# One subtraction of the first stage on VectorE instead of GpSimd, with the order of TensorE's groups written out anew

## The chip, the cores and the metric

The kernel runs on one core of one Trainium2 chip. The metric is the device time of one execution in microseconds. Comparisons are made with the median of several runs. TensorE is called PE, VectorE DVE, ScalarE ACT, GpSimd POOL and SyncE SP, as in the profile.

## The reference

One layer normalisation of `x` (2048 rows of 640) feeds attention with 32 heads of 20, and a parallel branch does a shifted mixer and an MLP:

```python
xn = _layernorm(x)
qkv = (xn @ wqkv) ...                       # q, k, v: 32 heads of 20
p = softmax(q @ k.T * 20 ** -0.5)
attn = (p @ v) @ wo
h  = gelu(_layernorm(x) @ w1)               # then its four column blocks are shifted by +1, -1, +2, -2 rows
x1 = x + shifted(h) @ w2
mlp = gelu(_layernorm(x1) @ w3) @ w4
out = x + attn + x1 + mlp
```

All of it is in float32.

## The kernel before

**Two parts for every factor.** To keep float32 precision with PE's faster reading of rounded values, each matmul factor is held as a high part (the rounded value) and a low part (the value minus the high part). A product is the sum of high times high, high times low and low times high. So each weight tile costs a copy that rounds it and a subtraction that makes the low part.

**The plan.** The Python code first lists all operations with an engine, an estimated cost, dependences and a key (a due time; the smallest ready key goes first on an engine). `Plan.schedule` then runs a list scheduler over them, and the instructions are emitted in its order, so each engine's queue has that order. An operation with `port=True` also takes a resource that the planner lends to DVE or POOL, one at a time, for the operation's planned length. PE's queue is ruled further by a string, `ORDER`, with one letter for each PE group: `m` for the score products whose row maxima are taken (two matmuls, tile `pm`, then two maxima on DVE, tile `mx`), `s` for the score products that go to the exponential (two matmuls, tile `s`, then two exponentials on ACT, tile `p`), `p` for the product of the exponentials with v (tile `pv`, eight matmuls), `d` for everything else (projections, mixer, MLP, transposes). The letters say which kind comes next; among the `d` groups the planner's keys decide. The string has 65 rows and 7059 letters: 4499 `d`, 1024 `m`, 1024 `s`, 512 `p`.

**The first stage** works on four blocks `tb` of 512 rows of `x`. For a block `norm_rows` takes the statistics of its four row tiles on DVE (`bn_a`, `mva`), then the inverse root on DVE and POOL (`rv_a` on DVE; `ry_a`, `rt_a`, `lnk` on POOL), and normalises the tiles in place, two on DVE and two on ACT (`xb`). The first block does this in two halves. `turn_tiles` transposes the tiles on PE (`tp`), copies the high part on ACT and subtracts on DVE to make the low part (`xT`). Then `twins` multiplies the first columns of the q and k weights with the block, the k sum on one half of PE's rows and the q sum on the other, in two turns; in the second turn the halves are swapped. Each turn has 15 pairs of matmuls: five with high weights and high rows, five with high weights and low rows, five with low weights. Between the turns stands a fence: a memset of a one-element tile (`scratch`, line 344) on POOL that waits for the end of the first turn and lets the second begin. The two sums go through ACT and DVE (`hl`), are placed by PE (`pk`) and stored.

**The weights of the first stage.** `load_w0` loads the first 128 columns of the k weights (`w_k`, e = 1) and of the q weights (`w_q`, e = 0), 640x128 held as 128x640, rounds them on ACT and makes the low part with a subtraction of two 128x640 operands. `split_wv` does the same for the first half of the v weights in five pieces (`wv`). `norm_rows` ties these low parts behind DVE's normalising of row tile 2 (`pl.behind`). On POOL the five `wv` subtractions have key -903, those of `w_k` and `w_q` -898. Four memsets (`vst`, key -140) fill gaps on POOL from there on.

Of the kernel before, what the change touches and what calls it, by code (L numbers as in the profile page):

```python
# [97 lines left out]
ORDER = (  # L98
    "dddddddddddddddddddddddddddddddddddddddddddddddddddddddddddddddddddddddddddddddddddddddddddddddddddddddddmmddd"
    "ddddddddddddddddddddddddddddddddddddddddddddddddddddddddddddmdddddddmddddmddddmddddmddddddmdddddddddddddddmddd"  # L100
    "dddmmdddddddmdddddmddddddddmdmddddddddddddddddddmdddddddddmdmmdddddddddddddddmdddddddddddmddddmmdddddddddddddd"
    "mdddddmddddddddmdddmmdddddddddddddddddddddmddddddddmdmmdddddddmddddddddddddddddddddmddmddmdddddddmdddddddddddd"
    "mdddddddddddsmmdddddddddddsddsdddddddsdmdddddddddmssddddddddmdsdddsdddmdddddsdmdsddppppddmsddmddsdmdsddsddmdds"
    "dddsdmdmddppppmddddmsdddsddddmdsdddsmdddsdmdsddddsmddsddmddmmppppmdsdddsdsdmdddmdsddmdddsmddddsdmddsdmddsddmdm"
    "ddmdpppsmspsmsmspmsmpsmspmsmpsmssmpmsmpsmddddsmddddmdddsdmdddsmdddsdmdddsdmddsdmddmddsppssmpsmmppmdddsddmddsdd"
    "dmddddmdspddmsdddddsdmdsdddddmddmppsmddddddddsmdddddddsmdddddsddmdddsddddmdmppmsdddddsddmdsddddmdddsmddddddsdm"
    "ddddsdddmdmppppsmddddsddmddsddddsdddmsddddddmsddddmdddddsmpmsmpppdsmdddsddddddmsdddddsmddddsddmddsdddmdddmdspp"
    "ppdmdsmdddddddsddmdddddmsddddddmsdddsdddmdddmppsdmdddddsdmddddsddmddsdmdddsdddmddsdddddmdmppsmdddddsdmddsddddd"
    "ddmsmdddddddsddddmddmddmppmsmppmdsdsdddmdsddddmsdddddmmsdddddddmsdddsddmsdddsppmspsmsddpdssmpdddppsddsddmdddsd"
    "ddsdmddddsmdddmddsdddmddsddmdddsppmmspppdmsddddmsdddsdmdsdddddmsmdddsdddmdsddsdddmddmdsppmsmsppmsdddmmpdpdsmdd"  # L110
    "ddmdsdddmddsddmddsdmdsdddmdsdddsddmddsddspsmpmspdmspdppdmdsddmddddmddddsdddsmddsddmddsdddsmdsddmddsdmppppmsddm"
    "dddddmsdddmdsdmdddsmddddmsdddmddsdmdddsddmppsmmppmsddddsdsmddddsdmddsdddmsddmddsdmdddspsmpsdmdddmdsddddsmppdmm"
    "sdpdpsdddsdsdddddmsddddsdddmsddddmdsddddmdsdddmddsppmmsmspppsmspsmddddmdsdmdddmddsddddmsdddmsddddmsdddmdsdddmd"
    "mppssppsmdddddpssmpmdddsdmdddsdmdddsddddsmddddmdsdddmdddsddsddmpppmsmpdddsmddddmddmddsdddddmsddddmdsddddmsdddd"
    "ddsmsmpsmpppsmspsddmdpmdsddmdsdddmsdddddmssdddddmddmdsddsddmddsdpsmmpppsdmddddsmdsdddmdsddmddsdsppppmsdddmsddd"
    "msdddmdsddmdddssdddddpsmmppmddsdmddmdddddsdmpdmsdddsdmsdddmdsddmddsdmdddsddsdmppppmsdddmdsddsddsdmddddddmsmddd"
    "ddddsmddddmsddsddmsmmpppmspsmspsmddddsmdddsdmpsmddddmddsdmdsddddmspsdmpsmdddsdddmsddsdmdddddmddsppppddsmddsddm"
    "dddsmddsddmdsdmddsddmdsdmddmdmppppssddmddddmsdddmdsdddddmsmddddsddmdddsmdddsddmdmppppmsddmdsdddmdsddmddsddmdds"
    "mdddmdsdddsdsddmpsmpsmpsmpmsddmdsddddsdddsdmdmdpppdsddmddsdddsmpmsddmdsddmdsdddsddmsdddmdsppsmmppmsdddmdsddmdd"
    "ddmdsddddmsmdddddsmddddmdsdddmddspsmmpppmdddmddsdddmsddddmsdddmsddmdsdddmddmsddddsdmddspmspssmpsmspsmsdpsmspms"  # L120
    "mpmspssmpssmpssmpmsspsmpssmpsmmppmsddddmddddmdddddddmmdddddsdddddddddddddddmsddsddddddddssdddmddddddmdsdddddsd"
    "dddmdmppppmdddsdddddddsmdmddddddsddmddddsdddddddddddddddsddddddddddddmsmddddddsddddmddddddddsddmddddddmddddspp"
    "ppdmdsddddsddddmsddddsdddddddddddddsdddddsdddmsddddddmmdddddddsdddmdddmddppdsppmdddddsdmddsddddddsmdsddddddsdd"
    "mdddddsdmppsdmddddddsdmdddddsddmpdmsddddddmddsddddddmspsmpsmspssmppsddddddddddddddddddddsspmmspsmmppmmddsddddd"
    "dmdddmsddddsmdmddddddmsdddmdsdddmddddmdsddmdddmsdddmddddsmddddmdsdmddddspppppmsdddddddmddsddmddsddmddsdddsmddd"
    "sddmddsddsddmddddmmppppmsdddmdddddsdmddsdmdddsmdddsdmdddsdmdddsdmdddsmpppmsdddsdmdsdddmdsdddmsdddsmdsddddmmppp"
    "msdpsmddsddmdsddmddsdmpppsmdddsdmdddsdmdddsdmdddsmdddsdmddsdmddsdmddsdddmmppppmdddmddddsddmddsddddssdddmdddsds"
    "ddmdddsddsdspppsmspmmsppsmdddsdmdddsdmdddsdmdddsmdddsdmdddsddmddsdddmdspdppmsddmdsdddmsddmdsddmdsdddmmppppmsdd"
    "sddmdsdddmdsdmdddsdddddmddddmmdddddddsmdppsdmdddsdmddsddsddmdddsdmpsmspssmppppmsddmdsddddmsdmdddsddmddsmdddsdm"
    "ddddsmddsddmdddmsppppdmdsdmdddsdmdddmdsdddddssmdddddsddmddsdmdddddsmmmppmpmmspsmspsmspsmspsmspsmspsmspssmpmsmp"  # L130
    "ddddsmdddmdddsdddddsmdddsdddmddmppsmdddddddddddsdddsdddmdddddsmddddddddsdddmddddddddsdddddmdddspmddsdpdsmdsddd"
    "ddddmddddmmdddddddddddddpppddmdddddddsddddddsmddddddmddddmdddddspsmdddsddddmddsddsddddmsdddddmddsdddmdddsddddd"
    "dddddddppppmsdddddmsddddsdmdddddsmdddddmsdddmddddddmdspmsppddmsdddddddmsddddddsdmddddddsdmddddddmdspdmdsddmddd"
    "ddsddddddmmdddddsddddddsddddmsppdmsmppsmspssmpmsspmsspmsddddddddssddddddddddddpmspssmpsmspsmspsmspsmdddddsspps"
    "sddddmdsddddmdmmddddddmdddmdddddddddmdddddmdddddddmsdddmdddmddddmdsddmdddddmddmddddmdsdddddmmddddsddmddsdppdmd"
    "dsddddmmpppmddsddmdddddmddsdmdddsmdddsdmddsdmddsdmddsddmdsppsmspppsmdddsdmdddsdmdddsdmdddsmdddsddmddsddmddsdds"
    "ddmpppssmpppmsddsddmddsddmddsdmddddsmdsdddmddsdmddddsmddddmsppppddmdmdddsddddsdmdsddddmsddmddsdsddddmsdddmdmdd"
# [1427 lines left out]
```

## Time and profile before

| | |
|---|---|
| median of three runs | 1871.93 us (1871.77 to 1875.42) |
| the profiled execution | 1870.62 us, of which the span is 1868.5 us |
| granted TensorE clock | 0.999 |
| PE | 1855.8 us busy, 99% of the span |
| DVE | 1550.7 us, 83% |
| ACT | 1337.8 us, 72% |
| POOL | 404.8 us, 22% |

The span runs from the first to the last instruction. In the views, a row of the timeline gives start and length in us, the engine, the line of the kernel, the operation, the tile written and the tile read, and in brackets how long the engine was idle before it and what ended that. The chain of waits follows the last instruction back to whatever released it, so its pieces add up to the span. Most operations are recorded at line 324, matmul groups at line 356, because a helper issues them.

### The profile page before, as it was taken

The page shows a single profiled execution, that of the slowest core. Times are in us where ns is not written, and L with a number is a line of the kernel's source. Part 1 is how long each engine was busy: PE and PEld are TensorE (multiplying, and loading weights), DVE is VectorE, ACT ScalarE, POOL GpSimd, SP SyncE. Part 2 cuts the span into 40 slices and gives each one's busy share as a digit, 9 for nine tenths or more (in the row PEclk, how much of TensorE's full clock was granted, in tenths as well). Part 3 has the DMA queues.
Part 4 walks back from the last instruction along what each step waited for, and adds up shares of the span by engine and source line. Part 5 has one row for each costly group of instructions (what it writes and reads, how often), then busy time and mean ns, then how long its engine had stood idle before and what let it go on. Part 6 is the DMA issues. An engine that isn't in the chain of part 4 may idle for free.

```text
span 1868.5 us, 44324 instructions
## 1 busy us (share of the span) xinstructions
PE 1855.8 (99%) x17233; PEld 1276.6 (68%) x17233; DVE 1550.7 (83%) x2739; ACT 1337.8 (72%) x2459; POOL 404.8 (22%) x620
## 2 busy tenths in 40 slices
PE   9999999999999999999999999999999999999998
PEld 7975776666666648676666756665776777775777
DVE  8989888888888999988788988778887888789724
ACT  5267777787877886677887677788677777778661
POOL 6001111321212213211213320111222122212211
PEclk9999999999999999999999999999999999999999
DMA  5664555536353475645345673434423242343402
GB/s 200 178 184 134 136 136 158 162 115 180 107 158 122 123 243 169 189 151 177 118 127 187 210 208 102 126 98 151 121 80 91 73 116 84 81 135 121 139 13 113
DMA packets 230360, 257.79 MB, mean 138 GB/s; under 512 B 60520, under 2 KB 175672, under 8 KB 228352
## 3 DMA queue, kind: packets, MB, share of 16 engines
q1 hardware_dynamic: 230152, 254.98, 45.7%
q8 instruction: 135, 2.21, 0.5%
q14 instruction: 73, 0.60, 0.1%
HBM read 151.64 MB, written 103.25 MB: 136 GB/s over the span
## 4 chain that ended last, share of the span: by engine, by line
PE 95%; DVE 2%; POOL 1%; DMA 1%; issue 0%; SPq 0%; ACT 0%; DVEq 0%; POOLq 0%; ACTq 0%
PE ps L356 26%; PE pv L356 25%; PE s L356 14%; PE pm L356 14%; PE psv L356 4%; PE pso L356 3%; PE ps_k L356 3%; PE ps_q L356 3%; DVE mx L324 1%; PE psl L356 1%; PE tz L324 1%; DMA wd_w<-ph_w 0%; PE pmt L356 0%; PE c_w L356 0%; PE tp L324 0%
## 5 line engine op out<-in xcount | busy, mean ns | idle before, releaser
L324 DVE TENSOR_REDUCE mx<-pm 128x1 f32<-128x512 f32 x2048 | 1282.2, 683 | 207.9 <-PE pm L356 192.9
L324 ACT ACTIVATE p<-s 128x512 f32<-128x512 f32 x2048 | 1080.8, 611 | 277.4 <-PE s L356 232.7
L356 PE MATMUL pv<-p,v 128*32 128x512 f32 x4096 | 493.7, 598 | 0.1
L356 PE MATMUL s<-zq,kpack 62*128 62x512 f32 x2048 | 443.4, 410 | 0.7
L356 PE MATMUL pm<-kpack,zq 60*128 60x512 f32 x2048 | 441.0, 409 | 1.6 <-DVE ob L324 1.6
L356 PE MATMUL ps<-xT,w_w 64*128 64x512 f32 x2040 | 322.8, 394 | 0.4 <-DVE mx L324 0.3
L356 PEld LDWEIGHTS s<-zq,kpack 62*128 62x128 f32 x2048 | 227.4, 185 | 128.2 <-ACT p L324 38.6
L356 PEld LDWEIGHTS pm<-kpack,zq 60*128 60x128 f32 x2048 | 228.3, 185 | 110.6 <-DVE mx L324 26.3
L356 PEld LDWEIGHTS pv<-p,v 128*32 128x32 f32 x4096 | 110.2, 109 | 225.0 <-issue 196.1
L356 PEld LDWEIGHTS ps<-xT,w_w 64*128 64x128 f32 x2040 | 212.9, 186 | 32.9 <-issue 2.1
L324 POOL TENSOR_TENSOR ob<-ob,obq 128x512 f32<-128x512 f32 x96 | 125.2, 1304 | 403.2 <-ACT obq L324 312.3
L356 PE MATMUL ps<-xT 64*128 64x320 f32 x1632 | 168.0, 307 | 0.0
L356 PEld LDWEIGHTS ps<-xT 64*128 64x128 f32 x1632 | 150.2, 186 | 9.0 <-issue 2.5
L356 PE MATMUL ps<-xT,gT 64*128 64x320 f32 x1152 | 119.1, 307 | 0.0
L324 ACT COPY obq<-pv 128x512 f32<-128x512 f32 x75 | 44.1, 588 | 103.8 <-PE pv L356 102.8
L356 PEld LDWEIGHTS ps<-xT,gT 64*128 64x128 f32 x1152 | 104.4, 186 | 6.2 <-issue 0.8
L344 POOL MEMSET scratch<- 1x1 f32 x134 | 12.1, 90 | 432.0 <-PE ps L356 206.3
L356 PE MATMUL psv<-wv,xT 64*128 64x320 f32 x960 | 92.1, 309 | 1.0 <-ACT xT L324 0.8
L356 PEld LDWEIGHTS psv<-wv,xT 64*128 64x128 f32 x960 | 80.9, 185 | 7.4 <-POOL scratch L344 1.2
L356 PE MATMUL ps_q<-xT,w_q 64*128 64x512 f32 x480 | 77.9, 393 | 0.0
L356 PE MATMUL ps_k<-xT,w_k 64*128 64x512 f32 x480 | 74.4, 394 | 0.0
L324 POOL TENSOR_TENSOR ph_w<-pr_w,ph_w 128x320 fp32r<-128x320 f32 (+2 forms) x48 | 36.7, 764 | 151.6 <-ACT ph_w L324 120.9
(171 smaller groups left out, 1360.9 us busy)
## 6 DMA issues: line engine op xcount, KB each, us to landing
zq<-qd SPq DMA_DIRECT2D x156, 80.0 KB
kpack<-kd SPq DMA_DIRECT2D x78, 160.0 KB
w_w<-wd_w SPq DMA_DIRECT2D x48, 256.0 KB
gd<-pre SPq DMA_DIRECT2D x8, 1536.0 KB
g<-gd SPq DMA_DIRECT2D x64, 192.0 KB
wd_w<-ph_w SPq DMA_DIRECT2D x34, 320.0 KB
xT<-wd_w SPq DMA_DIRECT2D x34, 320.0 KB
vd<-vst SPq DMA_DIRECT2D x32, 256.0 KB
```

The costliest lines, as they stand in the source:

```text
L324: o.insts = [getattr(e, m)(val(out), *[val(x) for x in ins], **{k: val(v) for k, v in kw.items()})]
L344: o.insts = [nc.gpsimd.memset(scratch.get(), 0.0)]
L356: o.insts = [nc.tensor.matmul(out.get(), lhsT.get(), rhs.get(), **kw) for out, lhsT, rhs, kw in products]
```

## The change

The subtraction that makes the low part of `w_q` is given to DVE instead of POOL, with DVE's planned cost; that of `w_k` stays on POOL. The key, the port flag and the tie behind the normalising of row tile 2 stay.

```diff
-        w0s.append(pl("pool", c_pool(640), "tensor_sub", w0[e][:, 1], raw, _f(w0[e][:, 0]), port=True))
+        w0s.append(pl("pool" if e else "dve", (c_pool if e else c_dve)(640), "tensor_sub", w0[e][:, 1], raw, _f(w0[e][:, 0]),
+                      port=True))
```

The planned costs are `c_pool(640)` = 2.11 * 640 + 145 = 1495 ns and `c_dve(640)` = 640 / 0.96 + 65 = 732 ns.

`ORDER` is also written out anew: 18 of its 65 rows differ. The counts of the four letters are the same; groups change places by a few letters. The first 232 letters are unchanged, and so are those from 640 to 1399 and all from 3900 on; the differences lie in between, most of them in letters 232 to 640 and 2420 to 2860. The first of the rows that differ and one from the middle, as examples:

```diff
-    "dddmmdddddddmdddddmddddddddmdmddddddddddddddddddmdddddddddmdmmdddddddddddddddmdddddddddddmddddmmdddddddddddddd"
...
+    "dddmmddddddddmddddmdddddmddddmddddddddddddddddddmdmdddddddddmmddddddddddddddmddddddddddddmddddmmdddddddddddddd"
...
-    "mpmspssmpssmpssmpmsspsmpssmpsmmppmsddddmddddmdddddddmmdddddsdddddddddddddddmsddsddddddddssdddmddddddmdsdddddsd"
...
+    "spmspssmpssmpssmpmsmpsmpssmpsmmppmsddddmddmdddddddddmmddddddsddddddddddddmdsdddsdddddmdddssdddddddddmdsdsddddd"
```

The number of separate runs of `p` goes from 258 to 259.

More of the change, by code (lines that the diff above doesn't have):

```diff
@@ L100 @@
     "ddddddddddddddddddddddddddddddddddddddddddddddddddddddddddddmdddddddmddddmddddmddddmddddddmdddddddddddddddmddd"
-    "dddmmdddddddmdddddmddddddddmdmddddddddddddddddddmdddddddddmdmmdddddddddddddddmdddddddddddmddddmmdddddddddddddd"
-    "mdddddmddddddddmdddmmdddddddddddddddddddddmddddddddmdmmdddddddmddddddddddddddddddddmddmddmdddddddmdddddddddddd"
-    "mdddddddddddsmmdddddddddddsddsdddddddsdmdddddddddmssddddddddmdsdddsdddmdddddsdmdsddppppddmsddmddsdmdsddsddmdds"
-    "dddsdmdmddppppmddddmsdddsddddmdsdddsmdddsdmdsddddsmddsddmddmmppppmdsdddsdsdmdddmdsddmdddsmddddsdmddsdmddsddmdm"
+    "dddmmddddddddmddddmdddddmddddmddddddddddddddddddmdmdddddddddmmddddddddddddddmddddddddddddmddddmmdddddddddddddd"
+    "mdddddmddddddddmdddmmddddddddddddddddddddddmdddmdddddmmddddddddddddmdddddddddddddddmdddmdddddddmdddddddddddddm"
+    "ddddmdddddddsmddddmddddddsddsddddddddsddsdmdddddddmsddddsddmdddsdddmdddddsdmppppdsddsdddmdmdddsddmsdddsddddmds"
+    "dddsdmdmddppppmddddmdsddsdddsdmddddsmddsdddmsddddsmddsddmddmmppppdmsddsddsdmdddmdsdmddddsmddddsdmddsdmddsddmdm"
     "ddmdpppsmspsmsmspmsmpsmspmsmpsmssmpmsmpsmddddsmddddmdddsdmdddsmdddsdmdddsdmddsdmddmddsppssmpsmmppmdddsddmddsdd"
@@ L110 @@
     "ddsdmddddsmdddmddsdddmddsddmdddsppmmspppdmsddddmsdddsdmdsdddddmsmdddsdddmdsddsdddmddmdsppmsmsppmsdddmmpdpdsmdd"
-    "ddmdsdddmddsddmddsdmdsdddmdsdddsddmddsddspsmpmspdmspdppdmdsddmddddmddddsdddsmddsddmddsdddsmdsddmddsdmppppmsddm"
-    "dddddmsdddmdsdmdddsmddddmsdddmddsdmdddsddmppsmmppmsddddsdsmddddsdmddsdddmsddmddsdmdddspsmpsdmdddmdsddddsmppdmm"
+    "ddmdsdddmddsddmddsdmdsdddmdsdddsddmddsddspsmpmspdmspdppdmdsddmddddmddddsdddsmddddsmddsdddsmdsddmddsdmppppmsddm"
+    "ddddmsdddmdsddmdddsmddddmdsddmddsdmdddsddmppsmmppmsddddsdsmddddsdmddsdddmsddmddsdmdddspsmpsdmdddmdsddddsmppdmm"
     "sdpdpsdddsdsdddddmsddddsdddmsddddmdsddddmdsdddmddsppmmsmspppsmspsmddddmdsdmdddmddsddddmsdddmsddddmsdddmdsdddmd"
-    "mppssppsmdddddpssmpmdddsdmdddsdmdddsddddsmddddmdsdddmdddsddsddmpppmsmpdddsmddddmddmddsdddddmsddddmdsddddmsdddd"
-    "ddsmsmpsmpppsmspsddmdpmdsddmdsdddmsdddddmssdddddmddmdsddsddmddsdpsmmpppsdmddddsmdsdddmdsddmddsdsppppmsdddmsddd"
+    "mppssppsmdddddpssmpmdddsdmdddsdmdddsddddsmddddmdsdddmdddsddsddmpppmsmpdddsmddddmddmddsdddddmsddddmddsdddmddsdd"
+    "ddsmsmpmspppsmspsdddmdpmsddmdsddmdsdddddsmsdddddmdmddsdddsdmddsdpsmmpppsdmdddsdmdsdddmdsddmddsdsppppmsdddmsddd"
     "msdddmdsddmdddssdddddpsmmppmddsdmddmdddddsdmpdmsdddsdmsdddmdsddmddsdmdddsddsdmppppmsdddmdsddsddsdmddddddmsmddd"
-    "ddddsmddddmsddsddmsmmpppmspsmspsmddddsmdddsdmpsmddddmddsdmdsddddmspsdmpsmdddsdddmsddsdmdddddmddsppppddsmddsddm"
+    "ddsmddddddmsdsdddsmmmpppmspsmspsmddddsmddddsmpsmddddmdsddmdsdddmdspsmpmsdddsdmdsdddddsmdddddmdsdppppdsmddddsdm"
     "dddsmddsddmdsdmddsddmdsdmddmdmppppssddmddddmsdddmdsdddddmsmddddsddmdddsmdddsddmdmppppmsddmdsdddmdsddmddsddmdds"
@@ L120 @@
     "ddmdsddddmsmdddddsmddddmdsdddmddspsmmpppmdddmddsdddmsddddmsdddmsddmdsdddmddmsddddsdmddspmspssmpsmspsmsdpsmspms"
-    "mpmspssmpssmpssmpmsspsmpssmpsmmppmsddddmddddmdddddddmmdddddsdddddddddddddddmsddsddddddddssdddmddddddmdsdddddsd"
[L122 to L125, printed above, removed]
+    "spmspssmpssmpssmpmsmpsmpssmpsmmppmsddddmddmdddddddddmmddddddsddddddddddddmdsdddsdddddmdddssdddddddddmdsdsddddd"
+    "ddmddmppppmsdddddddddmdsddsdddmddddmddddsdddddddddddddddsddddddddddddmsmddddddsddddmddddddddsddmddddddmddddspp"
+    "ppdmdsddddsddddmsdddddsdddddddddddsddddddsdddsmddddddmmdddsdddddddmddddmdpppmspsmddddddddsdddddddssmddddddddsd"
+    "mdddddmdsppsdmdddddsdmdddddddmdspmdsdddddmdddsddddddmspsmpsmspssmppsmddddddddddddddddddddspsmspsmmppmmddsddddd"
+    "mddddmsddddsmdmddddddmsdddmdsdddmddddmdsddmdddmsdddmddddsmddddmdsdmddddspppppmsdddddddmddsddmddsddmddsdddsmddd"
     "sddmddsddsddmddddmmppppmsdddmdddddsdmddsdmdddsmdddsdmdddsdmdddsdmdddsmpppmsdddsdmdsdddmdsdddmsdddsmdsddddmmppp"
@@ L130 @@
     "ddddsmddsddmdddmsppppdmdsdmdddsdmdddmdsdddddssmdddddsddmddsdmdddddsmmmppmpmmspsmspsmspsmspsmspsmspsmspssmpmsmp"
[L131 to L134, printed above, removed]
+    "ddddsmdddmdddsdddddsmdddsdddmddmppsmdddddddddddsdddsdddmdddddsmdddddddsdmdddddddddddsddddddddmspmdsddpdsmddsdd"
+    "dddmdddmdmddddpddddddddddppdddddmddddsddddddsmddddddmddddmdddddspsmdddsddddmddsddsddddmsdddddmddsdddmdddddsddd"
+    "dddddddppppmsdddddmsddddmdsdddddmsdddddmsddddmddsdddmdpmppsdddmsdddddmsdddddddsmdddddddsdmddddddmdspdmdsddmddd"
+    "ddsddddddmmdddddsddddddsddddmsppdmsmppsmspssmpmspsmsspmsddddddddssddddddddddddpmspssmpsmspsmspsmspsmdddddsspps"
     "sddddmdsddddmdmmddddddmdddmdddddddddmdddddmdddddddmsdddmdddmddddmdsddmdddddmddmddddmdsdddddmmddddsddmddsdppdmd"
```

## The prediction

> **What bounds the kernel now.** I read the page first, for the engine that is full and for the chain that ended last.
>
> ```profile
> span 1868.5 us, 44324 instructions
> PE 1855.8 (99%) x17233; PEld 1276.6 (68%) x17233; DVE 1550.7 (83%) x2739; ACT 1337.8 (72%) x2459; POOL 404.8 (22%) x620
> PE 95%; DVE 2%; POOL 1%; DMA 1%; issue 0%; SPq 0%; ACT 0%; DVEq 0%; POOLq 0%; ACTq 0%
> ```
>
> PE holds 95% of the chain. POOL is busy for 22% of the span and holds 1% of the chain, about 19 us, so an edit that takes 1.6 us of work off POOL matters only where that 1% lies. The busy time by stretch shows where PE is not full. The columns are the stretch, its length, then the busy time of PE, PEld, DVE, ACT and POOL, then clock, DMA share and GB/s.
>
> ```profile
> 15.00:20.00 5.00, 4.03 (x33) 3.15 (x34) 5.00 (x19) 0.15 (x1) 5.00 (x7) 1.00 1.04 389
> 20.00:24.00 4.00, 3.32 (x29) 2.44 (x29) 3.76 (x13) 0.87 (x2) 3.92 (x12) 1.00 0.10 39
> 24.00:28.60 4.60, 4.53 (x33) 3.37 (x29) 4.36 (x10) 4.60 (x10) 1.34 (x6) 1.00 0.25 91
> 28.60:36.00 7.40, 7.37 (x63) 5.93 (x63) 7.33 (x18) 3.36 (x6) 2.28 (x8) 1.00 0.24 88
> ```
>
> PE loses 0.97 us in the first of these stretches and 0.68 us in the second, and in both POOL is full. DVE is full as well. The chain of waits in order of time (start, length, what) says which of the two ends last there:
>
> ```profile
> 15.93 1.54 POOL w_k L324
> 17.47 1.50 POOL w_q L324
> 18.97 0.46 POOL vst L324
> 23.96 0.91 ACT xb L324
> 24.87 0.60 ACT hl L324
> 25.49 1.29 DVE hl L324 x2
> 26.78 1.80 DVE xT L324 x3
> 28.63 3.71 PE ps L356 x29
> ```
>
> POOL ends last, and the moved subtraction is on the chain with 1.50 us. After 28.63 the chain is PE.
>
> **The change part by part: the subtraction.** POOL's queue at this place, from the timeline, and the two waits of PE that end there:
>
> ```profile
> 17.41 1.56 POOL L324 TENSOR_TENSOR w_q<-wr_q,w_q 128x640 fp32r<-128x640 f32 x1
> 19.56 1.03 POOL L324 TENSOR_TENSOR ry_a<-rv_a,mhalf 128x4 f32<-128x4 f32 x1
> 20.52 0.54 POOL L324 MEMSET vst<- 128x512 f32 x1
> 20.98 0.09 POOL L344 MEMSET scratch<- 1x1 f32 x1
> 22.90 0.20 POOL L324 TENSOR_TENSOR lnk<-rn_a,lnk 128x4 f32<-128x4 f32 x1
> 19.03 0.50 PE L356 MATMUL ps<-xT,w_q 64*128 64x512 f32 x1 [0.81 <-POOL w_q L324]
> 20.06 0.39 PE L356 MATMUL ps<-xT,w_q 64*128 64x512 f32 x1
> 21.13 0.50 PE L356 MATMUL ps<-xT,w_q 64*128 64x512 f32 x1 [0.68 <-POOL scratch L344]
> ```
>
> Removed from POOL: one instruction of 1.56 us. Added to DVE: one of the same shape, both operands in SBUF. The trace has just one such on DVE, in a later phase:
>
> ```profile
> L324 DVE TENSOR_TENSOR w_w<-r_w,w_w 128x640 fp32r<-128x640 f32 x1 | 0.8, 826 | 0.6 <-ACT w_w L324 0.6
> 14.39 0.76 ACT L324 CAST w_q<-wr_q 128x640 fp32r<-128x640 f32 x1
> 13.81 1.60 DVE L324 TENSOR_TENSOR xT<-tp,xT 128x512 fp32r<-128x512 f32 x3
> ```
>
> So it costs 0.83 us on DVE. It can begin once ACT has rounded `w_q` (14.39 + 0.76 = 15.15) and DVE has finished the first block's `xT` (13.81 + 1.60 = 15.41), and then ends at 15.41 + 0.83 = 16.24. That is the early bound. In the late one it begins when POOL is through with `w_k` (15.93 + 1.54 = 17.47) and ends at 18.30. PE needs both low parts, so it goes on between 17.5 and 18.4 instead of at 19.03: a gain of 0.6 to 1.5 us. I take the late end, because the planner lends one port to DVE and POOL (`port=True`), and so either queues this operation on DVE as if it followed `w_k` or lets it run first and pushes `w_k` behind it.
>
> The row that bears on whether the two engines can overlap here is DVE's `rv_a`, which reads two operands in SBUF while POOL subtracts:
>
> ```profile
> 18.77 0.22 DVE L324 SCALAR_TENSOR_TENSOR rv_a<-mva 128x4 f32<-128x4 f32 x1
> 22.09 0.15 DVE L324 SCALAR_TENSOR_TENSOR rv_a<-mva 128x4 f32<-128x4 f32 x1
> ```
>
> The first took 0.22 us and ended at 18.99, just after POOL's `w_q` at 18.97; the second, with no such subtraction beside it, took 0.15. The Trainium skill, page "SBUF — State Buffer", section "SBUF: two separate sides", says that a DVE instruction with two SBUF inputs and a GpSimd one that reads SBUF use one shared port pair as an exclusive lock, each for its whole length. By that rule the subtractions of `w_q` and `w_k` follow one another whatever the queue, and PE's gain is at the small end, 0.6 to 0.7 us; without it the gain would reach 1.5 us. The trace agrees on this one row, no more.
>
> **The fence.** After the wait PE works to 20.06 + 0.39 = 20.45, which becomes about 19.8. The second turn needs the `scratch` memset, which stood at 20.98 behind `ry_a` and a `vst` memset. POOL is now free from 17.47, and the four `vst` memsets, 0.46 us each on the chain, 1.8 us together, fit where `w_q` and they stood. Then `scratch` is issued either ahead of `ry_a`, at about 19.9, or behind it at about 20.6, and PE's second turn starts 1.1 or 0.4 us earlier.
>
> **The normalising of the second block.** `rv_a` now has 0.83 us more of DVE's work ahead of it, so it ends at 19.4 to 19.8 rather than 18.99, and `ry_a` starts at 19.5 to 19.8, about where it did (19.56). Of the time between the end of `ry_a` and that of the last `lnk` (20.59 to 23.10, 2.5 us) three memsets took 1.4, which are now done before. So `lnk` is ready 0.9 to 1.2 us earlier, and with it ACT's `xb`, which ended at 23.96 + 0.91 = 24.87. ACT's `hl` waits for both this and PE's second turn, so it comes 0.4 to 1.1 us earlier, and all of the chain to 28.63 with it. I take 0.7. What hid nothing here is PE's own work: it was idle.
>
> **What DVE owes.** The added 0.83 us lies ahead of everything in DVE's queue, and DVE's idle time from 20 to 36 in the stretches above is 0.24 + 0.24 + 0.07 = 0.55 us. So up to 0.3 us must come out late. Where:
>
> ```profile
> 32.42 0.17 DVE L324 SCALAR_TENSOR_TENSOR rv_a<-mva 128x4 f32<-128x4 f32 x1
> 35.12 1.74 ACT L324 ACTIVATE xb<-xb,lnk 128x640 f32<-128x640 f32 x2 [4.04 <-POOL lnk L324]
> 36.76 1.04 ACT L324 CAST hl<-ps 128x512 fp32r<-128x512 f32 x2
> 37.35 1.29 DVE L324 TENSOR_TENSOR hl<-ps,hl 128x512 fp32r<-128x512 f32 x2 [0.82 <-ACT hl L324]
> 38.76 1.27 PE pk L356 x4
> ```
>
> The last block's `rv_a` follows its statistics on DVE, and `lnk`, ACT's `xb`, ACT's `hl`, DVE's `hl` and PE's `pk` follow it in a row, with PE at the end. If `rv_a` slips by 0.3, `pk` comes 0.3 later than before instead of 0.7 earlier. Against it: `hl` of the second block has the smaller key (-885 against -874 for `xb`), and PE delivers it earlier now, so the planner can put it ahead of the second `xb`. I keep 0.5 us of the 0.7.
>
> **The new order.** The work of the 7059 groups is the same. One more run of `p` costs what starting one costs:
>
> ```profile
> 671.21 0.99 PE pv L356 x8
> 697.41 1.85 PE pv L356 x16
> ```
>
> Two runs of one group are 2 x 0.99, one run of two is 1.85: 0.13 us. What the changed places do to waits the trace of before cannot show; it shows how much waiting there is to change. The letters from 232 to 640, 1399 to 2090, 2420 to 2860 and 3590 to 3900 hold all differences. The row that begins at 2420 has no `d` for a while, and the chain has no projection from 671 us on, which gives 0.277 us a letter (an estimate) and puts these places near 60 to 180, 390 to 580, 670 to 790 and 990 to 1080 us. The shares of the chain in the last three:
>
> ```profile
> by line: PE pv L356 25.2%; PE ps L356 19.3%; PE s L356 15.2%; PE pm L356 14.6%; PE ps_q L356 11.8%; PE ps_k L356 7.3%; DVE mx L324 2.1%; PE c_w L356 1.6%; DVE hlh L324 1.0%; DVE obq L324 0.6%; DVE pre L324 0.5%; PE pmt L356 0.5%; issue 0.3%
> by line: PE ps L356 40.3%; PE pv L356 25.7%; PE s L356 14.9%; PE pm L356 14.2%; PE tz L324 4.4%; PE pmt L356 0.7%
> by line: PE ps L356 34.9%; PE pv L356 26.9%; PE s L356 15.8%; PE pm L356 14.2%; PE tz L324 4.9%; DVE mx L324 1.9%; DVE x L324 1.1%; PE pmt L356 0.4%; issue 0.1%; DVE ry_c L324 0.1%; DVE rt_c L324 0.1%
> ```
>
> They were asked for 340 to 580, 690 to 800 and 990 to 1090 us. DVE holds 2.1 + 1.0 + 0.6 + 0.5 = 4.2% of 240 us = 10.1 us, nothing, and 3.2% of 100 us = 3.2 us: 13.3 us in all that a new order could take away or add to. I have no reason for a sign and take 0 as the likeliest.
>
> **The sum.** -0.5 + 0.1 = -0.4 us. The profiled execution took 1870.62 us, 1.31 us less than the median of the runs shown, so it would become 1870.2, and the median 1871.5 us. About 0.2%, 3.7 us, is what a measurement of this kernel can tell from no change.
>
> **The rivals.** *Faster, by the order.* Nothing in the first stage can reach 3.7 us, since PE's idle time from 15 to 28.6 is 0.97 + 0.68 + 0.07 = 1.7 us. But if the new order frees 40% of the 13.3 us that DVE holds in the rewritten stretches, 5.3 us, the time is 1866.2. For it: those waits are there, mostly for row maxima, and the order moves `m` against `s` and `d` in just these places. Against it: the differences are a few letters, and one of the three stretches has no such wait at all.
>
> *Slower, by a new bunch of maxima.* Where `m` groups come close together without `d` between them, DVE falls behind and PE waits for maxima. The trace has such a place (second row), and the price of both sides:
>
> ```profile
> 32.33 0.48 PE pm L356 x4
> 1281.04 5.73 DVE mx L324 x10
> ```
>
> Ten maxima, five `m` groups, hold the chain for 5.73 us, 1.15 a group, while PE needs 0.24 for the two matmuls of one (four take 0.48 in the first row); the loss is about 0.9 us a group. Five groups bunched like this in the row at 2420, where the new order has `s` ahead of `m` and pushes several `m` two to five letters back, cost 4.5 us: 1871.5 + 4.5 = 1876.0. It decides from four groups bunched in one place on (4 x 0.9 = 3.6 us). For it: there is no `d` there to cover anything. Against it: the counts are the same, and a bunch in one place loosens another.
>
> *DVE gives all of it back.* If the slip of `rv_a` reaches `pk`, the first stage ends 0.3 us later than before: 1872.4 with the run of `p`, still within 0.2%.
>
> **How the numbers follow.** The forecast holds with 0.37 and the give-back with 0.08: together 0.45 for within 0.2%. Faster by the order has 0.29, because there is more waiting to lose in these stretches than in an average one and the first stage points the same way. The new bunch has 0.26. The range runs from the full gain of the first stage and the freed waits (1871.9 - 1.1 - 5.3 = 1865.5) to the give-back with a bunch as long as the one shown, 5.7 us without deduction (1872.4 + 5.7 = 1878.1, rounded to 1878.0). The likeliest case alone spans 1870.5 to 1872.5.
>
> **What would show it.** Right: `w_q` on DVE with 0.8 to 0.9 us, not overlapping a subtraction on POOL; PE goes on at about 18.3; `scratch` before 20.7; the chain's PE part begins at about 27.9 instead of 28.63. Wrong in the first stage: `rv_a` of the second block after 20, or `pk` later than 38.8. For the rest, DVE's share in the three stretches of the chain says which case it is: clearly under 13.3 us for faster, a run of ten or more `mx` near 670 to 700 us for slower. A change of more than 2 us that appears before 60 us would refute the reasoning altogether.

## The result, and the profile after

The changed kernel is slower by about 0.2%: 1876.74 us against 1873.22 us, both the median of 20 runs; the ratio is 1.002 (95% interval 1.0014 to 1.0027). The forecast was 1871.5 us from 1871.93, no difference that can be measured. The profiled execution after took 1873.88 us with a span of 1871.6; before it was 1870.62 us and 1868.5. Both lie below the medians of their runs, by 2.9 and 2.6 us, so the two profiles differ by about as much as the medians do. One execution of the kernel before here (2228.62 us), and one each in two of the later comparisons, took far longer than all others; they are left out of the ratios and ranges.

The page of the changed kernel, answering the first lines of the prediction:

```profile
span 1871.6 us, 44328 instructions
PE 1859.0 (99%) x17233; PEld 1279.9 (68%) x17233; DVE 1553.5 (83%) x2745; ACT 1336.9 (71%) x2457; POOL 400.7 (21%) x616
PE 93%; DVE 4%; DMA 2%; POOL 0%; issue 0%; SPq 0%; ACT 0%; DVEq 0%; ACTq 0%; POOLq 0%
```

POOL has left the chain, as intended. DVE went from 2% to 4% and DMA from 1% to 2%. One per cent is 19 us, far more than the loss of 3 us, so these shares show over which engines the chain now runs and not how much was lost. The busy time by stretch in the first stage of the changed kernel (columns as before), and behind it the row of the kernel before that was not shown yet:

```profile
15.00:20.00 5.00, 4.48 (x34) 3.17 (x34) 5.00 (x16) 0.15 (x1) 4.67 (x9) 1.00 1.04 395
20.00:24.00 4.00, 3.98 (x33) 3.17 (x34) 3.92 (x14) 1.40 (x2) 2.01 (x6) 1.00 0.20 73
24.00:28.60 4.60, 4.49 (x28) 3.04 (x28) 4.60 (x12) 4.60 (x10) 2.19 (x7) 1.00 0.37 138
28.60:36.00 7.40, 7.40 (x65) 5.88 (x62) 6.66 (x17) 2.14 (x4) 1.88 (x6) 1.00 0.16 58
36.00:45.00 9.00, 8.13 (x53) 5.39 (x51) 7.76 (x16) 8.42 (x16) 3.19 (x3) 1.00 0.44 148
```

```profile
36.00:45.00 9.00, 9.00 (x66) 6.93 (x65) 8.00 (x19) 7.75 (x16) 2.90 (x1) 1.00 0.42 151
```

PE is fuller up to 24 us (4.48 and 3.98 for 4.03 and 3.32) and then loses 0.87 us in 36 to 45, where it had been full.

To see where the rest went, each matmul of one profile is set beside the same one of the other (the n-th of its kind); the difference of their start times is called the offset here, positive where the kernel is behind the profile of before. The changed kernel is 0.6 us ahead at 28 to 36 us, 1.2 behind at 46 to 318, 0.2 behind at 340, 0.7 ahead at 1040, and then falls back in steps: 0.5 behind at 1072, 1.3 at 1090, 2.4 at 1105, 3.1 at 1130 and 3.4 at the end. So two places lose: 36 to 45 us, and 1050 to 1130 us with 3.7 us. The second lies in the last of the rewritten stretches of the order and just behind it. The chain of waits there in the changed kernel (start, length, what):

```profile
1063.56 1.13 DVE mx L324 x2
1065.43 0.91 DVE x L324 x2
1066.35 0.60 DVE obq L324
1066.95 0.61 DVE mx L324
1070.44 0.09 POOL scratch L344
1076.75 5.25 DMA md<-mT
1082.07 2.65 DMA zq<-md
```

And from the waits of PE and the timeline of DVE, first the kernel before, then the changed one:

```profile
1066.48 0.59 ACT L324 COPY obq<-pv 128x512 f32<-128x512 f32 x1
1096.69 0.69 DVE L324 COPY ob<-pv 128x512 f32<-128x512 f32 x1
1099.60 0.33 DVE L324 CAST ph_wo<-pr_wo 128x320 fp32r<-128x320 f32 x1 [0.98 <-DMA wd_wo<-ph_wo]
```

```profile
PE s L356 <- DVE ob L324: 0.7, 1, 0.7
PE s L356 <- DMA zq<-md: 0.4, 1, 0.4
1066.26 0.68 DVE L324 COPY obq<-pv 128x512 f32<-128x512 f32 x1
1099.50 0.33 DVE L324 CAST ph_wo<-pr_wo 128x320 fp32r<-128x320 f32 x1 [1.50 <-DMA wd_wo<-ph_wo]
1099.74 0.68 DVE L324 COPY ob<-pv 128x512 f32<-128x512 f32 x1
1124.91 0.68 DVE L324 COPY pre<-ps 128x512 f32<-128x512 f32 x1
```

Nothing of this is in the diff as such. The planner chooses for some operations between ACT and DVE or POOL and DVE, and it sets the order on each engine; with the new letters it gave two evacuations of PSUM, `obq` and `pre`, to a DVE that was busy for 9.9 to 10.0 of 10 us there in the kernel before, put `ob` behind a cast that waits for a store to land, and on POOL put `rb` ahead of a fence (below).

### The profile page after: what moved, and what is told of

Same layout as the page of the kernel before. It is cut to its first block, busy times and chain, and to the rows that moved or that the text cites. A ratio compares the mean times of both kernels' runs of the same rounds, so it can differ in the third digit from the quotient of the medians.

```text
span 1871.6 us, 44328 instructions
## 1 busy us (share of the span) xinstructions
PE 1859.0 (99%) x17233; PEld 1279.9 (68%) x17233; DVE 1553.5 (83%) x2745; ACT 1336.9 (71%) x2457; POOL 400.7 (21%) x616
## 4 chain that ended last, share of the span: by engine, by line
PE 93%; DVE 4%; DMA 2%; POOL 0%; issue 0%; SPq 0%; ACT 0%; DVEq 0%; ACTq 0%; POOLq 0%
PE ps L356 26%; PE pv L356 24%; PE s L356 14%; PE pm L356 14%; PE psv L356 4%; PE pso L356 3%; PE ps_q L356 3%; PE ps_k L356 3%; DVE mx L324 1%; PE psl L356 1%; PE tz L324 1%; DVE xT L324 0%; DVE bn_a L324 0%; DMA wd_w<-ph_w 0%; PE pmt L356 0%
```

## The experiments

The theory at this point: the late loss comes from the letters of the last stretch, by way of what the planner makes of them on the other engines; the first stage costs little. The rivals: the moved subtraction costs it all, or the places of the groups on PE do.

This table holds the steps of the offset in every profile against the one of before, in us: from 16 to 46-56 us (*first stage*; the input's own delay is taken off so), across 327 us (from 310 to 340), then around 1061, 1066-1071, 1084, 1098 and 1125 us, and the ratio of the times with its interval (8 to 12 runs of each kernel, one run of e9 and of e10, against 23 to 35 of the kernel before). A positive step is time lost.

| kernel | first | 327 | 1061 | 1066 | 1084 | 1098 | 1125 | ratio |
|---|---|---|---|---|---|---|---|---|
| changed | 1.0 | -1.0 | 0.28 | 0.92 | 0.75 | 1.07 | 0.53 | 1.0020 (1.0014-1.0027) |
| e1 move only | 1.0 | 0.0 | 0.00 | -0.02 | -0.11 | -0.35 | -0.03 | 1.0006 (0.9994-1.0018) |
| e2 order only | 0.0 | -0.6 | 0.27 | 0.92 | 0.72 | 0.92 | 0.53 | 1.0006 (0.9995-1.0018) |
| e3 changed, old late rows | 1.1 | -1.3 | 0.00 | -0.01 | 0.12 | 0.54 | -0.04 | 0.9999 (0.9989-1.0010) |
| e4 before, new late rows | 0.0 | 1.1 | 0.25 | 0.93 | 0.39 | 0.72 | 0.53 | 1.0018 (1.0004-1.0032) |
| e9 before, 73 new letters | 0.0 | -0.8 | -0.01 | -0.03 | -0.12 | -0.37 | 0.00 | one run |
| e10 before, 166 new letters | 0.0 | -1.4 | 0.26 | 0.00 | 0.28 | 3.33 | 0.00 | one run |
| e11 evacuations on ACT | 1.0 | -1.0 | 0.27 | 0.93 | 0.37 | 0.13 | 0.00 | 1.0012 (1.0000-1.0025) |
| e12 before, evacuations on DVE | 0.0 | -1.3 | 0.01 | 0.59 | 6.76 | -0.13 | 0.52 | 1.0031 (1.0017-1.0044) |
| e14 `ob` ahead of the cast | 1.0 | -1.3 | 0.21 | 0.92 | 0.67 | -0.35 | 0.51 | 1.0005 (0.9994-1.0017) |
| e15 three undone | 1.0 | -0.8 | 0.26 | -0.01 | 1.65 | -0.22 | 0.02 | 1.0013 (1.0002-1.0024) |
| e7 `vst` late | 2.8 | 1.4 | -0.02 | -0.01 | -0.12 | 3.42 | 0.00 | 1.0011 (0.9998-1.0023) |
| e8 maxima held | 0.7 | -0.4 | 0.00 | 0.00 | 0.40 | 3.74 | -0.01 | 1.0007 (0.9995-1.0018) |
| e13 `vst` behind `xb` | 1.8 | -1.3 | 0.01 | -0.01 | -0.12 | 0.47 | 0.00 | 0.9997 (0.9987-1.0007) |
| e16 maxima held, `xb` early | 0.4 | -1.0 | 0.00 | -0.02 | 0.74 | 3.75 | -0.04 | 1.0014 (1.0001-1.0026) |
| e17 before, `ob` first at 327 | 0.0 | -1.1 | 0.02 | -0.02 | -0.09 | 0.02 | -0.01 | 1.0007 (0.9998-1.0016) |
| e18 e3, `ob` first at 327 | 1.0 | -0.6 | -0.02 | 0.00 | -0.04 | -0.35 | 0.00 | 1.0014 (1.0005-1.0024) |

Some columns repeat from kernel to kernel to within 0.1 us (first, 1061, 1066, 1125): they hang on the order of instructions. Others (327, 1084, 1098) end in the landing of a transfer and differ by microseconds between executions; e1 and e16 have the same late letters, and at 1098 the one gains 0.35 and the other loses 3.75. The largest of these steps have a second part: behind the wait the granted TensorE clock falls to half for some us (e4 and e7 at 327, e12 at 1084, e7, e8, e10 and e16 at 1098; the section on the hardware shows e16).

**Which part: e1 to e4.** e1 and e2 take one half of the change each:

```diff
 # e1: the changed kernel
-ORDER = (the new rows)
+ORDER = (the rows of before)
 # e2: the kernel before
-ORDER = (the rows of before)
+ORDER = (the new rows)
```

> The subtraction is on VectorE, the string ORDER is that of before. Theory (two separate costs: the first stage loses 1.2 us by 45 us because VectorE's queue puts two maxima ahead of the fourth block's rv_a, and the span loses 4 us between 1056 and 1128 us because of the rewritten letters 3590 to 3900): the first stage is as in after (the fourth block's rv_a at 33.9, PE's product after it at 43.7), but the late loss is absent, so ratio to before 0.999 to 1.001. Rival (the moved subtraction alone costs the time, whatever the order): 1.0014 to 1.0027, as after.

> The subtraction is on GpSimd as before, the string ORDER is that of after. Theory (the loss is in the rewritten order): ratio 1.001 to 1.003, the first 45 us as before (fourth block's rv_a at 32.4), and waits of PE for row maxima or DMA between 1056 and 1128 us. Rival (the moved subtraction): 0.999 to 1.001.

Neither alone is told from the kernel before (1.0006 each), but the profiles separate them cleanly: the move alone has the first stage's 1.0 us and none of the late steps, the order alone has all the late steps and nothing in the first stage. By the times alone e2 missed its expectation: 1.0006 lies in the range that was its rival's, though the interval reaches 1.0018. e3 and e4 exchange only the rows 33 to 36 of the order, the last rewritten stretch:

```diff
 # e3: the changed kernel
-rows 33 to 36 of ORDER: the new ones
+rows 33 to 36 of ORDER: those of before
 # e4: the kernel before, the exchange the other way
```

> As after, but rows 33 to 36 of ORDER (letters 3520 to 3960) are those of before. Theory (the late letters hold the loss): ratio to before 0.999 to 1.0005, with the first stage still 1.2 us behind at 45 us and caught up by 335 us. Rival (the late loss follows from what came earlier, a planned time that has slipped, and the letters only go with it): 1.0014 to 1.0027.

> As before, but rows 33 to 36 of ORDER (letters 3520 to 3960) are those of after. Theory (the late letters hold the loss): ratio to before 1.0015 to 1.0025, with about 4 us lost between 1056 and 1128 us and nothing before. Rival (they only go with a loss made elsewhere): 0.9995 to 1.0005.

e3 is level with before (0.9999) and e4 is slower alone (1.0018). The loss comes with these four rows. How much of it is open: e4's interval begins at 1.0004, and e2, which has the same rows, came out at 1.0006.

**Which letters: e9 and e10.** These rows differ in two clusters. e9 takes the letters 3590 to 3663 of the new order into the kernel before, e10 the letters 3734 to 3900.

```diff
 # e9: the kernel before
-letters 3590 to 3663 of ORDER: those of before
+letters 3590 to 3663 of ORDER: the new ones
 # e10: the same with letters 3734 to 3900
```

> As before, with letters 3590 to 3663 of ORDER from after. Theory (the steps lost between 1058 and 1128 us come from the letters that are run just ahead of them, 3734 to 3900): no step over 0.3 us there. Rival (they come from the earlier cluster, which shifts the plan): steps of 1.0, 0.5, 0.8 and 0.6 us as in after.

> As before, with letters 3734 to 3900 of ORDER from after. Theory (these letters cost the time): four steps of about 1.0, 0.5, 0.8 and 0.6 us between 1058 and 1128 us, together 3 us. Rival (letters 3590 to 3663): none.

Neither cluster alone makes the steps at 1066 and 1125 us; in both kernels `obq` stays on ACT. It takes both together, as in e4 (one profile each), and how the planner comes to its choice was not followed further.

**The evacuations: e11 and e12.** e11 keeps the two on ACT in the changed kernel, e12 puts them on DVE in the kernel before.

```diff
-def evac(o, ps, n):
-    pl("act", c_act(n), "copy", o, ps, dk=K_FE, alt=("dve", ...) if A_EV else None)
+def evac(o, ps, n, pin=False):            # pin: obq of block 17, second quarter; pre of half 1, f 1, b 1
+    pl("act", c_act(n), "copy", o, ps, dk=K_FE, alt=("dve", ...) if A_EV and not pin else None)   # e11
+    # e12, where pin is set: pl("dve", c_dve(n), "tensor_copy", o, ps, dk=K_FE)
```

> The changed kernel with two PSUM evacuations kept on ACT: obq of block 17, second quarter (near 1066 us), and pre of half 1, f 1, second column block (near 1125 us). Both are on DVE in the changed kernel and on ACT in the one before. Theory: these two, 0.68 us each on a DVE that is full there, make the steps of 1.2 us between 1056 and 1076 and of 0.7 us between 1112 and 1128; so both steps are gone, those at 1084 and 1097 to 1104 (landings of stores, 0.7 and 1.1 us) may stay, and the time against before falls from a ratio of 1.002 to about 1.001. Rival: the letters themselves (or the landings) make the steps; then they stay and the ratio stays near 1.002.

> The kernel before, order and first stage unchanged, with the same two evacuations put on DVE. Putting the first there also moves the cast ph_wo ahead of ob near 1100 us, as in the changed kernel. Theory: the steps appear without any new letter, 1.2 us between 1056 and 1076 and 0.7 us between 1112 and 1128, and about 1 us more near 1100 from the cast that now stands ahead of ob: 2 to 3 us in all, ratio 1.001 to 1.0016, nothing before 1050 us. Rival (the letters make the steps): no step, ratio within 0.0005 of 1.

Half of the theory held. The step at 1125 us is `pre` on DVE: gone in e11 (0.00), there in e12 without a new letter (0.52). The step at 1066 us appears in e12 with 0.59, but it stays whole in e11 (0.93). The waits of PE from 1050 to 1135 us and POOL's timeline in e11 say why:

```profile
PE ps L356 <- POOL scratch L344: 0.7, 1, 0.7
1068.47 1.31 POOL L324 TENSOR_TENSOR ob<-ob,obq 128x512 f32<-128x512 f32 x1
1069.72 1.31 POOL L324 TENSOR_TENSOR rb<-ob,rb 128x512 f32<-128x512 f32 x1
1070.95 0.09 POOL L344 MEMSET scratch<- 1x1 f32 x1
```

The fence between two turns of matmuls stands behind `rb`, 1.31 us long, which in the kernel before ran only at 1077 us. PE can't pass 1070.95 in any case; in the changed kernel half of the 0.92 us is spent earlier, waiting for the maximum behind `obq`, and half at the fence, and with `obq` off DVE the fence takes all of it. Two limits that end together: to remove one gains nothing. In e12 the cast `ph_wo` did move ahead of `ob`, but the step expected from that at 1098 didn't come (-0.13): PE was 7 us late there, and DVE no longer had to wait for the landing. e12's ratio, 1.0031, is far over the 1.001 to 1.0016 expected; the two steps explain 1.1 us of it, and the 6.76 us at 1084 are taken up in the section on the hardware.

**The landing in front of `ob`, and all at once: e14 and e15.** e14 exchanges two instructions of DVE in the changed kernel; e15 adds to that the pins of e11 and a tie of `rb` behind the fence.

```diff
     evac(obs[blk], pvs[blk], 512)
+    if blk == 18:
+        casts["wo_3_1"].deps.append((pl.ops[-1], 1))       # e14, e15: the cast ph_wo behind ob
...
+rbs[16].deps.append((fences["ps2_15_0"], 1))               # e15: rb of block 16 behind the fence
```

> The changed kernel with one exchange in DVE's queue: the evacuation ob of block 18 (near 1099 us) stands ahead of the cast ph_wo, which waits until an earlier store has landed (1.50 us in the profile of the changed kernel). Theory: PE's wait for ob, 0.7 us, is gone and with it 0.7 to 1.1 us of the time, so the profiled offset at the end falls from 3.4 to 2.3 to 2.7 us over before. Rival: the wait for the store is only moved to another group (the maxima behind it), and the step between 1090 and 1104 us stays at 1.1.

> The changed kernel, its letters untouched, with three things put back at once: the two evacuations (obq of block 17, pre) on ACT, rb of block 16 on POOL behind the fence (scratch) that it stood ahead of at 1069 us, and ob of block 18 ahead of the cast ph_wo. Theory: the late loss comes from what the planner does on DVE and POOL for the new letters, in three places, and the first two of them end at nearly the same time near 1070 us, so that one alone brought nothing; with all back, the offset over before grows by at most 1.0 us between 1050 and 1130 us (0.3 from a slow scratch at 1061, up to 0.7 from the load of zq at 1084) instead of 3.7 in the changed kernel, and the ratio is 1.000 to 1.0005. Rival: the places of the s, m and p groups themselves cost the time; then at least 2.5 us of the 3.7 stay and the ratio stays near 1.0015 to 1.002.

In e14 `ob` is done before the landing, and PE's wait is gone:

```profile
1097.47 0.69 DVE L324 COPY ob<-pv 128x512 f32<-128x512 f32 x1
1099.31 0.32 DVE L324 CAST ph_wo<-pr_wo 128x320 fp32r<-128x320 f32 x1
```

The step at 1098 goes from 1.07 to -0.35, more than the 0.7 to 1.1 expected. The ratio is 1.0005 for the changed kernel's 1.0020, more than a step of 1.4 us (0.0008) explains, and the two intervals overlap: that this exchange alone brings the time back isn't shown, and e15, which has it too, came out at 1.0013. In e15 the letters are all new and the steps at 1066, 1098 and 1125 us are gone, so it was not the places of the groups on PE. Its expectation of at most 1.0 us of growth failed, though: 1.9 us are left, 1.65 of them at 1084, and the ratio, 1.0013, lies between theory and rival. This is what is left, from e15's chain and waits of PE (the fence's memset took 0.39 us at 1061 for 0.09 in the kernel before; why wasn't tried):

```profile
1061.29 0.39 POOL scratch L344
1076.04 5.19 DMA md<-mT
1081.29 3.38 DMA zq<-md
PE s L356 <- DMA zq<-md: 1.3, 1, 1.3
```

`zq` is read back after `md` has landed. The loads of `xT` queued between the two on SP are two in the kernel before and four with the new letters (both in the changed kernel and in e15), and the landing took 2.65 and 3.38 us there against 1.59 in e16, with the old letters. Against the loads as the whole reason: the longest landing, 4.38 us, is e12's, which has the old letters and three such loads there. That the loads make the difference wasn't tried. With intervals of 0.001 the experiments don't settle how the remaining 0.001 is split between this load and the wait at 1098.

**The first stage: e7, e13.** Would POOL's new room help if the `vst` memsets stood aside? e7 and e13 try that on the kernel before.

```diff
-        pl("pool", 500.0, "memset", v, 1.0).deps.append((wvs[-1], 0))
+        pl("pool", 500.0, "memset", v, 1.0).deps.append((nbs[2], 1))     # e7: behind the last lnk of the second block
+        pl("pool", 500.0, "memset", v, 1.0).deps.append((xdv[-1], 1))    # e13: behind DVE's second xb of that block
```

> As before (w_q on GpSimd, ORDER of before), but the four vst memsets may not start until the second block's last lnk, so that they no longer stand between ry_a and lnk on GpSimd. Theory (the memsets' 1.4 us in the normalising chain can be had without any work added to VectorE): lnk of the second block ready about 1 us earlier, PE 0.4 to 1.0 us earlier than before from 28 to 300 us with nothing given back at 45 us. Rival (any gain by 30 us is given back by the fourth block, since VectorE is full): level with before or later at 45 us. Ratio 0.998 to 1.001 in either case, since the wait for a store near 320 us can take the gain.

> The kernel before with the four vst memsets tied behind DVE's second xb of the second block, so that they can't run beside it. In the run with the memsets held until the last lnk, two xb of DVE took 2.97 us while the memsets ran beside them. Theory of the shared port: with no memset beside them the two xb take 1.1 to 1.2 us, lnk of the second block comes 1 to 1.5 us earlier than in the kernel before and PE is 0.5 to 1 us ahead at 28 us. Rival: something else held the xb (the late input rows, for one); then they take clearly over 1.2 us again. Past 331 us the gain is expected to be gone in either case, ratio within 0.0008 of 1.

`lnk` came earlier in both, and the time didn't follow: with the input's own delay taken off, PE is 1.0 us behind at 28 us in e7, where 0.4 to 1.0 ahead was expected, and level in e13. DVE's two `xb` and the memsets beside them, in the kernel before, e7 and e13, from the timelines:

```profile
22.85 1.14 DVE L324 TENSOR_SCALAR xb<-xb,mva,lnk 128x640 f32<-128x640 f32 x2 [0.21 <-POOL lnk L324]
```

```profile
21.36 2.97 DVE L324 TENSOR_SCALAR xb<-xb,mva,lnk 128x640 f32<-128x640 f32 x2 [0.26 <-POOL lnk L324]
21.53 1.94 POOL L324 MEMSET vst<- 128x512 f32 x4
```

```profile
21.69 2.04 DVE L324 TENSOR_SCALAR xb<-xb,mva,lnk 128x640 f32<-128x640 f32 x2 [0.27 <-POOL lnk L324]
21.86 1.00 POOL L324 MEMSET vst<- 128x512 f32 x2
```

The tie of e13 rules the planner's times and no semaphore, and two of the memsets still ran beside the `xb`, so its expectation of 1.1 to 1.2 us wasn't met. It shows the more: with none, two and four memsets the pair took 1.14, 2.04 and 2.97 us, that is 0.90 and 1.83 more for 1.00 and 1.94 us of memsets. In these rows the DVE operation is held up for about as long as POOL writes. The Trainium skill, page "SBUF — State Buffer", section "SBUF: two separate sides", calls the port pair that DVE and GpSimd share "an exclusive lock, not a bandwidth split"; these rows agree with it.

**The first stage: e8, e16.** Why is the changed kernel 1.0 us behind at 46 us, when `pk` (38.17 for 38.70) still was 0.53 ahead? The fourth block in the changed kernel, by the timelines of DVE, ACT and PE:

```profile
32.65 0.68 DVE L324 TENSOR_REDUCE mx<-pm 128x1 f32<-128x512 f32 x1
33.35 0.64 DVE L324 TENSOR_REDUCE mx<-pm 128x1 f32<-128x512 f32 x1
33.91 0.15 DVE L324 SCALAR_TENSOR_TENSOR rv_a<-mva 128x4 f32<-128x4 f32 x1
38.03 3.07 DVE L324 TENSOR_TENSOR xT<-tp,xT 128x512 fp32r<-128x512 f32 x5
41.02 0.60 DVE L324 TENSOR_SCALAR xb<-xb,mva,lnk 128x640 f32<-128x640 f32 x1
40.88 1.00 ACT L324 ACTIVATE xb<-xb,lnk 128x640 f32<-128x640 f32 x1
41.68 1.53 PE L324 MATMUL tp<-ident,xb 128*128 128x128 f32 x12 [0.46 <-DVE xb L324]
```

`rv_a` is at 33.91 for 32.42. Two maxima stand ahead of it, and the `xb` behind it have fallen behind `hl` and five `xT`; PE waits for them with the transposes. e8 holds the maxima of the first four `m` groups behind `rv_a`, e16 also lowers the key of the fourth block's `xb`; both have the old late rows of e3.

```diff
+            if j < 4:
+                o.deps.append((rvs[-1], 0))      # e8, e16: o is the maximum of unit j
...
+        if ts[0] == 12:
+            pl.key -= 16                         # e16: the xb of the fourth block
+            d += 16
```

> As e3 (subtraction on VectorE, late rows of ORDER from before), but the first four maxima may not start before the fourth block's rv_a. Theory (what the first stage loses comes from the two maxima that VectorE's queue put into the 0.13 us holes ahead of rv_a, and from xb of the fourth block being queued behind hl and xT because of that): rv_a at 32.7 instead of 33.9, PE at 45 us between 0.6 us earlier and 0.3 us later than before, instead of 1.2 to 1.9 us later. Rival (the subtraction's own 0.83 to 1.09 us on a full VectorE is the loss, wherever the maxima stand): still 1 us or more later at 45 us. Ratio to before 0.998 to 1.0005.

> The changed kernel with the old letters near 1050 us, the first four maxima held behind the last rv_a of the first stage (as in an earlier run), and the normalising xb of the fourth block with a key 16 lower, so that ACT's xb of the last row tile stands ahead of xT of the third block. Theory: the other part of the loss of the first stage is this xb behind hl and five xT on ACT; then PE at 45 us is level with before or up to 0.5 us ahead of it (apart from a late start of the input), where it was 0.7 us behind with the maxima alone held. Rival: DVE's 0.8 us more work sets the end whatever the order; then PE stays 0.5 us or more behind.

Behind at 46 us were 1.1 us in e3, 0.7 in e8 and 0.4 in e16. So the maxima explain about 0.4 us and the order of `xb` another 0.3. e8 lies between its theory (at most 0.3 behind) and its rival (1 or more). The rest, from e16's timelines:

```profile
32.81 0.16 DVE L324 SCALAR_TENSOR_TENSOR rv_a<-mva 128x4 f32<-128x4 f32 x1
35.49 1.74 ACT L324 ACTIVATE xb<-xb,lnk 128x640 f32<-128x640 f32 x2 [5.27 <-POOL lnk L324]
38.48 0.66 PE L324 MATMUL tp<-ident,xb 128*128 128x128 f32 x4 [1.13 <-DVE hl L324]
```

`rv_a` is 0.39 us later than in the kernel before and so is all behind it, up to PE at 46 us (0.4). With the order put right, this is what is left of the move; no run takes DVE's added work away and keeps the rest, so that it is this work is argued. It is what the rival of e16 said, at a smaller size than the 0.5 it named.

**The wait at 327 us: e17 and e18.** Both profiles have a wait for a landing in front of another `ob`, 1.6 us on PE before and 0.5 after, and the offset falls there from 1.2 to 0.2. Is the first stage's loss taken up by it?

```diff
+    if blk == 4:
+        casts["w2_1_1"].deps.append((pl.ops[-1], 1))    # e17: the kernel before; e18: e3
```

> The kernel before with the evacuation ob of block 4 ahead of the cast ph_w2_1_1, which waits near 327 to 330 us for a store to land (2.31 us in the profile of before; PE then waits 1.6 us for ob). The planner then gives ob to ACT. Theory: this wait is on PE's path in the kernel before, and it is also what takes up the 1.2 us lost by the first stage of the changed kernel; without it the time falls by about 1.5 us, ratio 0.9990 to 0.9995. Rival: the landing holds other work just behind (the cast's subtraction, maxima) and the time stays, ratio 0.9997 or over.

> The changed kernel with the old letters near 1050 us and the same exchange near 327 us (ob of block 4 ahead of the cast). Theory: without the wait at 327 us nothing takes up the loss of the first stage any more, so this kernel is 0.5 to 1.5 us slower than the kernel before with the same exchange, that is level with the kernel before (0.9995 to 1.0002). Rival: the loss is taken up elsewhere, and it is as fast as the kernel before with the exchange.

e17 gains the 1.1 us at 327, and loses more behind: 2.2 us at 348 to 356, where the planner now gives DVE two subtractions of `hlh` that POOL had and PE waits 1.0 us for the cast behind them, and 4.1 us from 885 on, where PE waits 1.8 us for a maximum and the granted clock falls to half behind it. It is not faster (1.0007). e18 stands 0.0007 above e17, on the side of the theory, but within what the runs can tell. And the table speaks against it: across 327 us the offset also falls in e2, e9, e10 and e12, which have no loss to take up. The landing there is late by different amounts in different executions: PE waits 1.6 us for this `ob` in the kernel before and in e1, and 0.2 us in e3, e10, e12 and e13. That the loss is taken up isn't shown.

## Why the prediction was wrong, point by point

*The subtraction*: right in the time. `w_q` stood on DVE from 17.18 for 1.09 us and PE went on at 18.33, as forecast (about 18.3). The sign named for it, 0.8 to 0.9 us without overlap, failed: it overlapped `w_k` by 0.42 us and took 0.26 more than the 0.83 of its row, and the two misses cancel in its end (18.27 for 18.30), which is luck.

```profile
16.02 1.58 POOL L324 TENSOR_TENSOR w_k<-wr_k,w_k 128x640 fp32r<-128x640 f32 x1
17.18 1.09 DVE L324 TENSOR_TENSOR w_q<-wr_q,w_q 128x640 fp32r<-128x640 f32 x1
19.87 0.09 POOL L344 MEMSET scratch<- 1x1 f32 x1
20.02 0.49 PE L356 MATMUL ps<-xT,w_q 64*128 64x512 f32 x1 [0.26 <-POOL scratch L344]
```

*The fence*: right, at the early end of its two (19.87), and PE's second turn came 1.1 us earlier. *The normalising of the second block*: right in size; the offset at 28 to 36 us is -0.6 for the -0.7 taken. On the way `rv_a` ended at 20.06 instead of 19.4 to 19.8 (the sign of being wrong was "after 20"), and `lnk` was ready 0.5 us earlier instead of 0.9 to 1.2.

*What DVE owes*: wrong, mis-sized. The debt was put at up to 0.3 us and watched at `pk`, which indeed stayed ahead. It came out one step further, at the transposes of the fourth block. Of the 1.8 us that PE falls back from 28 to 46 us, 1.2 stay in e16, with the order put right, and the planner's gaps, filled with maxima, and `xb` put behind `hl` and `xT` make the other 0.6. The prediction named that exchange of `hl` and `xb` as a reason to keep the gain; it did not ask who waits for `xb`. Where the sum gave back 0.2 us and kept 0.5, the kernel gave back 1.8 and ended 1.0 behind. The chain says the same: its part on PE was to begin at about 27.9, but it still runs over DVE here:

```profile
41.10 0.53 DVE xb L324
```

*The new order*: this is the step that failed and carries the sign. It was taken as 0, with the run of `p` at 0.13, because no sign could be read from the letters; in the last rewritten stretch it cost 3.7 us in the profile, and with the old letters there (e3) the ratio is 0.9999. Of the 3.7 us 1.7 (0.28 + 0.92 + 0.53) follow from the instructions' order and came back in e2 and e4 alike; 1.8 are two waits for landings. The middle stretches gained 0.8 us (from 0.16 behind at 340 to 0.68 ahead at 1040), so "no sign" was fair for them. The prediction's own sign shows it: DVE's share of the chain in the three stretches is 10.1 + 0 + 8.4 = 18.5 us for the 13.3 before, the growth all in the last. What failed is how the change was read: the changed letters were read as work on PE that moves a little, and the price was looked for in maxima; the mechanism that decided, the planner re-choosing engine and place of evacuations, fences and casts on full engines, was among neither the terms nor the rivals. e15 shows it for three of the five steps in the profile; its time, 1.0013 (1.0002-1.0024), leaves open how much of the loss they are. The rival of a new bunch of maxima near 670 to 700 us did not occur: the chain has no maxima there in either kernel. That the measured 1876.74 us lies near the 1876.0 of that rival is luck.

## What the runs showed of the hardware

A short wait of PE can cost about double. In e16 PE waits 1.8 us for a maximum near 1101 us; the busy times by stretch behind it (the third column from the right is the granted clock):

```profile
PE pm L356 <- DVE mx L324: 1.8, 1, 1.8
1103.00:1104.00 1.00, 0.85 (x6) 0.56 (x8) 1.00 (x3) 0.00 (x0) 0.11 (x1) 1.00 0.73 192
1105.00:1106.00 1.00, 1.00 (x10) 0.35 (x10) 0.00 (x0) 0.52 (x2) 0.00 (x0) 0.50 1.06 307
1107.00:1108.00 1.00, 1.00 (x8) 0.20 (x4) 0.00 (x0) 0.54 (x2) 0.00 (x0) 0.51 0.88 293
1108.00:1109.00 1.00, 1.00 (x10) 0.27 (x4) 0.00 (x0) 0.06 (x1) 0.00 (x0) 1.00 0.42 129
```

The clock is at half for three us or a little more, and the step is 3.75 us. e17 lost 4.1 us to a wait of 1.8 us in the same way, and e12's 6.76 us at 1084 are a wait of 4.0 us for `zq` and then the clock at about half from 1086 to 1093. The length of the wait doesn't decide alone: waits of 1.4 and 1.5 us near 330 us were followed by the clock at 0.50 in e4 and e7, while 1.6 us at the same place left it at 1.00 in the kernel before and in e1. e1, e11 and e14 lost 1.2 us near 1292 us, with the clock at 0.50 for some us and no wait of PE over 0.3 us in the 10 us ahead of it, where the changed kernel kept 1.00. A wait of 0.7 us (the changed kernel, near 1099) left the clock at 1.00. The Trainium skill, page "TensorE: Matmul & The Clock Gate", section "HAM oscillation — how this bites in real kernels", gives the rule as "no PE-idle gaps >~3.4µs"; here 1.8 us were enough. Executions of one kernel lie up to 0.5% apart, from 1869.0 to 1878.1 us for the kernel before in the last comparison; there the seven with a granted clock of 1.000 over the whole took 1871.6 us on average and the sixteen with 0.997 or 0.998 took 1874.3. Landings that differ, with such a clock behind some of them, are the likeliest reason, but not shown. The clock isn't what makes the changed kernel slower: its seven runs with 1.000 took 1875.3 us on average.

## What to carry to other kernels

Where a planner re-derives the whole program, price an edit by what else it will re-decide: compare the instruction order of each engine before and after, and look first at optional placements on engines that have no idle time and at queue heads that wait for a landing. Work moved onto a full engine comes out at some waiter; follow each operation that slips to everyone who reads it, beyond the first one. And when undoing a suspect changes nothing, look for a second limit that ends at the same time before you acquit it.
